# A planned attention-and-FFN kernel: the plan's count for transposing DMAs, and a new order of loads and bursts

## The chip, the cores and the metric

The kernel runs on one core of one Trainium2 chip. The metric is the device time of one execution in microseconds (us), the median of several runs. A profile of one of these executions gives the times of single instructions.

## The reference

Two layers follow each other: an attention whose softmax is replaced by a squared ReLU, and a gated FFN.

```python
B, H, S, D = 8, 12, 448, 64
scores = (q @ k.transpose(0, 1, 3, 2)) / sqrt(D)
attn = maximum(scores, 0) ** 2 / S
x = (attn @ v).transpose(0, 2, 1, 3).reshape(3584, 768)
gate = maximum(x @ w_gate, 0)          # w_gate, w_val: 768 x 1536
val = x @ w_val
out = (gate * val) @ w_out             # w_out: 1536 x 768; out: 3584 x 768, float32
```

## The kernel before, in words

All matrix work is done in bf16 with float32 sums in PSUM. The attention goes by quads: four heads of one batch, so three quads a batch and 24 in all. A quad needs q and k with the head dimension on partitions. For batch 0 (L494, L501) and batch 1 (L527) PE transposes them. For batches 2 to 7 it goes through DMA: a raw tile is loaded from DRAM by a queue that POOL issues (L394), one engine copies it into a permuted tile (L550, mostly DVE), and SP issues two transposing DMAs from there into a tile qkT (L556). There is one raw tile and one permuted tile. So the next raw load waits for the copy before it, and the next copy waits for the two transposes before it.

The scores of a quad are made in steps (L622), four 64x64 matmuls a step that run side by side in the four quarters of the array. ACT or DVE applies the ReLU (L631, L633) and the square (L643, L645). Then PE makes attention times v (L661, 28 matmuls; "PV"), and a copy (L676) puts the result into xT, the FFN's input.

The FFN of batches 0 and 1 is plain: 30 blocks of a gate product and a value product (L721, six matmuls each), a ReLU on ACT (L729) and a multiplication on DVE that writes hT (L731). From batch 2 on, and for every output product, pairs of batches are multiplied by a Strassen scheme with seven products instead of eight (L821 for gate and value, L936 for the output). It needs sums and differences of the weights, which DVE makes once: L744 and L749 from the gate and value weights, L761 from the output weights, into tiles woT and wo. The scheme also needs copies of partial results, tiles f (L770, L772), which DVE adds in again (L849, L871, L887, L926). Results leave through tiles o and DMAs that SP issues (L908).

No loop runs in this order. The function `plan` (L161) takes the operations of all stages and simulates the engines with fixed costs; what it starts first is emitted first. Each engine then runs its instructions in that order, and an instruction that waits holds up all behind it on the same engine. PE's operations come in two lists, `att` and `ffn`, each with its own order, and the planner mixes them: a run of attention between FFN products is a burst here. It starts one when the FFN work done since has reached a share (`START`, or `LATEST` at the latest) of what the ratio of the two lists asks for. While PE waits in the first 21 us, the planner puts in filler matmuls (L1065) whose results nobody reads. POOL's loads have a fixed order, spelled by `ORDER`: V is v of batch 0, L the late part of its q, a digit a pair of gate and value columns, a letter of abcxyz a quad of batches 1 and 2 with its v, a letter of opqr a quarter of w_out.

The planner has one number for the DMA queue, `dmaq`: the time at which it comes free. A load adds its transfer time. A transposing operation (`xbar`) adds a constant, and its end is bounded from the queue's:

```python
if op.xbar:
    self.dmaq = max(self.dmaq, s) + 1.5
    op.end = max(op.end, min(self.dmaq + 2.0, s + 13.0))
```

`LATE` is added to that end for whoever uses the result. `BUFFERS` gives the numbers of the tiles qkT, at, xT, f, g, o and vv.

Of the kernel before, what the change touches and what calls it, by code (L numbers as in the profile page):

```python
# [15 lines left out]
class Res:  # L16


    def __init__(self, n):
        self.free = {i: 0.0 for i in range(n)}  # L20
# [35 lines left out]
class Planner:  # L56
# [1 line left out]
    SWITCH = 0.1  # L58
    BIAS = 0.2
    MARGIN = 4.0  # L60
    LATE = 3.0
    RESERVE = (1000.0, 12.0, 2.0)
    FILL_FROM = 0.4
    FILL_COLD = 4.0
    FILL_UNTIL = 21.0
    FILL_MARGIN = 0.1
    WINDOW = 5
    ATT_WINDOW = 2
    START = 0.8
    LATEST = 3.0  # L70
    HOLD = 0.1
    SLACK = 0.1
    CUTS = ((1, 3), (0, 1, 3, 5, 6), (2, 6), (2, 6))
    GV_ORDER = '1256734'
    OUT_ORDER = 'ab1cd572364'
    END_ORDER = ('517364', '523')
    BUFFERS = (3, 11, 3, 5, 4, 5, 3)
    PV_AT_0 = 1
    QT = 3
    PART = 6  # L80
    PV_AT = 1
    T_AT = 3
    MORE_UNTIL = 4
    BY_PE = 6
    ORDER = 'VL102acbx34y5zroqp'

    def __init__(self, banks):
        self.banks = banks
        self.t = {}
        self.ops = []  # L90
        self.mode = None
        self.dmaq = 0.0
        self.landed = []
# [7 lines left out]
    def ready(self, op):  # L101
        r = 0.0
        for d in op.deps:
            if d.end is None:
                return None
            if d.eng != "PE" or "PE" not in op.engs:
                r = max(r, d.end + (self.LATE if d.xbar else 0.0))
        for b in op.alloc:
# [22 lines left out]
    def commit(self, op, s, e):  # L131
        op.start, op.eng = s, e
        occ, busy = op.engs[e]
        now = self.now(op)
        self.t[e] = s + occ
        op.end = s + busy
        if e == "PE":
            self.mode = op.mode
        if op.load:
            self.dmaq = max(self.dmaq, s + occ + 0.3) + op.load  # L140
            op.end = self.dmaq + 2.0
            self.landed.append(op.end)
        op.end += op.land
        if op.xbar:
            self.dmaq = max(self.dmaq, s) + 1.5
            op.end = max(op.end, min(self.dmaq + 2.0, s + 13.0))
        for b in op.alloc:
            b.idx = b.pick(now)[1]
            for w in range(b.width):
                del b.res.free[b.idx + w]  # L150
            b.last = op.end
        for b in op.reads:
            b.readers -= 1
            b.last = max(b.last, op.end + (self.LATE if op.land else 0.0))
            if b.readers == 0:
                for w in range(b.width):
                    b.res.free[b.idx + w] = b.last
        self.ops.append(op)


def plan(first, att, ffn, others, pool, goals, filler, banks):  # L161
# [33 lines left out]
    def fits(ops, now):  # L195

        among, width = ops[0].alloc[0].among, ops[0].alloc[0].width
        times = sorted(max(P.free_at(i + w) for w in range(width)) for i in among)
        for o, t in zip(ops, times):
            if t > now + P.SLACK:  # L200
                return False
            now += o.engs["PE"][0]
        return True

    first = [list(x) for x in first]
    while any(first) or att or ffn or active or pi < len(pool):
# [18 lines left out]
        else:  # L225
            A = F = None
            for i, op in enumerate(att[:P.ATT_WINDOW]):
                b = P.best(op)
# [10 lines left out]
            elif A is not None and F is not None:  # L239
# [3 lines left out]
                else:  # L243
                    n = next((i for i, o in enumerate(att) if o.cut), len(att) - 1) + 1
                    if debt >= P.LATEST * n * share:
                        pick = "A" if A[0] <= F[0] + 0.15 else "F"
                    elif debt >= P.START * n * share and A[0] <= now + 0.15 and fits(att[:n], now):
                        pick = "A"
# [50 lines left out]
def kernel(  # L299
# [40 lines left out]

    N_QT, N_AT, N_X, N_F, N_G, N_O, N_VV = Planner.BUFFERS
    N_RAW, N_PERM = 1, 1
# [194 lines left out]
    def transpose_dma(b, g):  # L537
        st = quads[(b, g)]
        st.qt_buf = Buf(r_qt)

        pb = Buf(r_perm)
        perm = Op({"DVE": (0.65, 0.72), "ACT": (2.1, 2.2)}, None, deps=st.qk_ops, alloc=[pb],
                  reads=[st.raw_buf] if st.raw_buf else [])

        def emit_perm():
            src = st.raw().rearrange("p (j h) t d -> p j t h d", j=2)
            if perm.eng == "ACT":
                nc.scalar.copy(perm_t[pb.idx], src)
            else:
                nc.vector.tensor_copy(perm_t[pb.idx], src)  # L550

        perm.emit = emit_perm

        def emit():
            for a in range(2):
                nc.sync.dma_start_transpose(out=qkT_t[st.qt_buf.idx][:, a].rearrange("p j (t c) -> p (j t) c", c=P2),  # L556
                                            in_=perm_t[pb.idx][64 * a:64 * a + 64].rearrange("p j t h d -> p (j t h d)"))

        op = Op({"SP": (2.6, 2.6)}, emit, deps=[perm], alloc=[st.qt_buf], reads=[pb])
        op.land = 7.4 if b == 2 else 5.4  # L560
        op.xbar = True
        st.qt_ops = {0: [op]}
        others.extend([perm, op])
# [515 lines left out]
    out_of = dict(zip("opqr", [(par, hf) for par in range(2) for hf in range(2)]))  # L1079
    for x in Planner.ORDER:  # L1080
        if x in "VL":
# [19 lines left out]
    def T(n):  # L1101
        if n < Planner.BY_PE:
            att.append(transpose_pe(*divmod(n, NQ)))
        elif n < B * NQ:
            transpose_dma(*divmod(n, NQ))

    def PV(n):
        att.append(A_[n].pv())
        if A_[n].g == NQ - 1:
            done_at[A_[n].b] = len(att)  # L1110
# [10 lines left out]
    for n in range(NQ, len(A_)):  # L1121
# [3 lines left out]
        for i in range(len(A_[n].steps)):  # L1125
            att.append(A_[n].s(i))
            if i == (Planner.PV_AT if n >= 2 * NQ else Planner.PV_AT_0) and n not in (NQ, 2 * NQ):
                PV(n - 1)
            if i == Planner.T_AT and n >= 2 * NQ - 1:
                T(n + 1 - NQ)  # L1130
# [51 lines left out]
```

## Time and profile before

| What | Value |
|---|---|
| median of 6 runs | 412.7 us |
| lowest and highest run | 410.65 and 415.64 us |
| the profiled execution | 415.3 us, with a span of 413.5 us from first to last instruction |
| PE busy | 398.3 us (96% of the span), 3481 matmuls |
| DVE busy | 324.4 us (78%) |
| ACT busy | 257.3 us (62%) |
| POOL busy | 74.2 us (18%) |
| loads' queue | 23.60 MB, 43.6% of 16 engines' span |
| stores' and transposes' queue | 19.08 MB, 27.9% |
| transposing DMAs | 36, two for each of 18 quads; issue to landing 3.3 / 6.6 / 14.4 us (least, median, most) |

Lines such as L821 are lines of the kernel before. "PE ps L821" is a matmul there that writes the tile ps. "A <- B" means that A waited and B ended the wait. A busy PE in this profile is not a PE at its peak: matmuls are pipelined and overlap in the record, so what one of them takes is read from the length of a row of them.

### The profile page before, as it was taken

The numbers are of one execution on the slowest core, as the hardware profiler recorded it, in microseconds if no ns is written. First come the engines' busy times: TensorE is split into PE (matmuls) and PEld (weight loads), VectorE is DVE, ScalarE is ACT, GpSimd is POOL, SyncE is SP. The second block draws the span as 40 slices with busy tenths as digits, with TensorE's granted clock in tenths as the row PEclk, the third lists the DMA queues.
The fourth block names the chain that finished last, engine by engine and source line by source line (L and its number), as shares of the span: only waits on it lengthen the run. The fifth ranks groups of instructions, "written<-read, shape, count | busy, mean of one in ns | idle before, by whom it ended". The sixth has DMA issues, their size and how long they took to land.

```text
span 413.5 us, 8787 instructions
## 1 busy us (share of the span) xinstructions
PE 398.3 (96%) x3481; PEld 207.0 (50%) x3481; DVE 324.4 (78%) x573; ACT 257.3 (62%) x385; POOL 74.2 (18%) x119
## 2 busy tenths in 40 slices
PE   8979999979999999999999999999999999999995
PEld 4567644433455544444545544444445555555563
DVE  3697979957899988899698699898788757767652
ACT  3888878543677777788587389756575544343221
POOL 7827405201211222221112022210000000000000
PEclk9999999998999999999999999999999999999998
DMA  8999999996479999766879699831002440000144
GB/s 110 189 198 202 179 135 153 176 158 90 69 90 184 142 192 145 104 72 92 101 90 158 124 189 135 111 38 31 2 0 65 99 106 2 1 0 2 38 110 120
DMA packets 75736, 43.43 MB, mean 105 GB/s; under 512 B 37808, under 2 KB 75696, under 8 KB 75696
## 3 DMA queue, kind: packets, MB, share of 16 engines
q0 software_dynamic: 33328, 23.60, 43.6%
q1 hardware_dynamic: 42208, 19.08, 27.9%
q8 instruction: 27, 0.44, 0.5%
q10 hardware_dynamic: 160, 0.20, 0.1%
q14 instruction: 13, 0.11, 0.1%
HBM read 47.19 MB, written 11.01 MB: 141 GB/s over the span
## 4 chain that ended last, share of the span: by engine, by line
PE 78%; DMA 10%; issue 4%; DVE 3%; POOL 2%; ACT 1%; DVEq 0%; POOLq 0%
PE ps L821 35%; PE ps L936 23%; PE ps L622 7%; PE ps L661 6%; PE ps L721 6%; DMA wo<-in_moe_w_out_dram 5%; DMA wg<-in_moe_w_gate_dram 2%; DMA gvT<-in_k_dram 2%; POOL gvT L394 1%; DMA raw<-in_k_dram 1%; DVE at L633 1%; DVE at L645 1%; ACT at L631 1%; POOL wo L394 1%; DMA out_dram<-o 1%
## 5 line engine op out<-in xcount | busy, mean ns | idle before, releaser
L631 ACT ACTIVATE at<-ps 128x896 bf16<-128x896 f32 (+3 forms) x111 | 97.4, 911 | 21.1 <-PE ps L622 20.7
L770 ACT COPY f<-ps 128x448 f32<-128x448 f32 x99 | 51.8, 532 | 47.0 <-PE ps L821 45.6
L633 DVE TENSOR_SCALAR at<-ps 128x896 bf16<-128x896 f32 (+4 forms) x60 | 63.0, 1051 | 12.1 <-PE ps L622 11.6
L645 DVE TENSOR_TENSOR at<-at 128x896 bf16<-128x896 bf16 (+4 forms) x118 | 69.4, 610 | 4.0 <-ACT at L631 3.5
L821 PE MATMUL ps<-xT,gvT 128*128 128x448 bf16 x216 | 52.6, 353 | 0.0
L643 ACT ACTIVATE at<-at 128x896 bf16<-128x896 bf16 (+4 forms) x53 | 49.7, 939 | 4.1 <-DVE at L633 3.4
L821 PE MATMUL ps<-sx,wv 128*128 128x448 bf16 x216 | 52.2, 353 | 0.0
L622 PE MATMUL ps<-qkT 64*64 64x448 bf16 (+2 forms) x756 | 49.7, 337 | 2.1 <-DMA qkT<-perm 1.1
L821 PE MATMUL ps<-xT,wg 128*128 128x448 bf16 x216 | 51.6, 353 | 0.0
L821 PEld LDWEIGHTS <-gvT 128*128 128x128 bf16 x324 | 30.4, 98 | 32.0 <-issue 5.4
L936 PE MATMUL ps<-wo,hT 128*128 128x384 bf16 x240 | 43.9, 326 | 0.1
L936 PEld LDWEIGHTS <-hT 128*128 128x128 bf16 x312 | 29.7, 98 | 22.9 <-issue 3.9
L394 POOL DMA_DIRECT2D vv<-in_v_dram x44 | 26.7, 621 | 77.9 <-PE ps L622 75.4
L936 PEld LDWEIGHTS <-sh 128*128 128x128 bf16 x288 | 27.0, 98 | 21.3 <-issue 3.7
L721 PE MATMUL ps<-xT,wg 128*128 128x448 bf16 (+2 forms) x180 | 33.6, 324 | 4.2 <-DVE hT L731 3.8
L772 ACT ACTIVATE f<-ps 128x384 f32<-128x384 f32 x39 | 19.0, 491 | 28.6 <-PE ps L936 28.6
L661 PE MATMUL ps<-at,vv 64*64 64x448 bf16 (+2 forms) x700 | 33.7, 329 | 0.0
L721 PE MATMUL ps<-xT,wv 128*128 128x448 bf16 (+2 forms) x180 | 32.8, 319 | 0.8 <-DVE at L633 0.8
L394 POOL DMA_DIRECT2D raw<-in_k_dram x18 | 11.3, 628 | 117.6 <-DVE perm L550 98.9
L861 DVE TENSOR_TENSOR hT<-ps,g 128x448 bf16<-128x448 f32 x36 | 22.4, 622 | 12.1 <-PE ps L821 12.1
L676 ACT CAST xT<-ps 128x896 bf16<-128x896 f32 (+2 forms) x27 | 22.2, 821 | 14.8 <-PE ps L661 13.0
L622 PEld LDWEIGHTS <-qkT 64*64 64x64 bf16 x756 | 17.5, 105 | 27.4 <-issue 21.9
(63 smaller groups left out, 484.6 us busy)
## 6 DMA issues: line engine op xcount, KB each, us to landing
out_dram<-o SPq DMA_DIRECT2D x110, 96.0 KB, 2.2
vv<-in_v_dram POOLq DMA_DIRECT2D x44, 112.0 KB, 6.1
raw<-in_k_dram POOLq DMA_DIRECT2D x18, 224.0 KB, 5.1
raw<-in_q_dram POOLq DMA_DIRECT2D x18, 224.0 KB, 6.7
wg<-in_moe_w_gate_dram POOLq DMA_DIRECT2D x6, 384.0 KB, 9.6
wv<-in_moe_w_val_dram POOLq DMA_DIRECT2D x6, 384.0 KB, 10.9
wo<-in_moe_w_out_dram POOLq DMA_DIRECT2D x4, 576.0 KB, 15.8
gvT<-in_k_dram POOLq DMA_DIRECT2D x6, 224.0 KB, 6.4
```

The lines of the kernel that those rows point to most:

```text
L394: op = Op({"POOL": (0.5 + 0.0004 * n_desc,) * 2}, lambda: nc.gpsimd.dma_start(out=dst(), in_=src), deps=deps, alloc=alloc)
L622: nc.tensor.matmul(banks()[64 * j:64 * j + 64, z, h2], lhsT=self.k_of(j, h2, k), rhs=self.q_of(j, h2), start=True, stop=True)
L631: nc.scalar.activation(self.at_of(i, m), banks(), AF.Relu)
L633: nc.vector.tensor_scalar_max(self.at_of(i, m), banks(), 0.0)
L643: nc.scalar.activation(a, a, AF.Square)
L645: nc.vector.tensor_tensor(a, a, a, ALU.mult)
L661: nc.tensor.matmul(ps[64 * h2:64 * h2 + 64, ps2.idx + j, :n], lhsT=st.v_of(j, h2, c), rhs=self.at_of(c)[64 * j:64 * j + 64, 0, h2], start= ...
L721: nc.tensor.matmul(ps[:, pb.idx, :n], lhsT=w[:, kd, fc], rhs=xT_t[xbuf[b].idx][:, kd, cols], start=(kd == 0), stop=(kd == KD - 1))
L770: nc.scalar.copy(dst, src)
L821: nc.tensor.matmul(ps[:, pb.idx, :S], lhsT=w(g)[:, fc], rhs=rhs, start=start and g == 0, stop=stop and g == KH - 1, skip_group_check=True)
L861: h0 = Op({"DVE": V448}, lambda pb=prev["A"], gb=prev["g0b"], mf=prev["mf"]: nc.vector.tensor_tensor(h_slot(b, mf), ps[:, pb.idx, :S], g_t ...
L936: nc.tensor.matmul(ps[:, pb.idx, :OH], lhsT=lhs(kf), rhs=rhs(kf), start=start and kf == 0, stop=kf == FH - 1, skip_group_check=True)
```

## The change

The constants for the transposing DMAs are new, and the plan's other constants are set anew: how bursts are started (`ATT_WINDOW`, `START`, `LATEST`), when PE's transposes stand among the score steps (`T_AT`), the numbers of the tiles, and the order of the loads. POOL is taken as free from 1.25 us on. The arithmetic that the kernel does is the same. Below L142 the lines of the changed kernel are one higher.

```diff
-    LATE = 3.0
+    LATE = 2.0
...
-    ATT_WINDOW = 2
-    START = 0.8
-    LATEST = 3.0
+    ATT_WINDOW = 3
+    START = 0.9
+    LATEST = 1.8
...
-    BUFFERS = (3, 11, 3, 5, 4, 5, 3)
+    BUFFERS = (3, 11, 3, 3, 5, 5, 4)
...
-    T_AT = 3
+    T_AT = 0
...
-    ORDER = 'VL102acbx34y5zroqp'
+    ORDER = 'LV021abc3x4yo5zqpr'
...
-        self.t = {}
+        self.t = {"POOL": 1.25}
...
         if op.xbar:
-            self.dmaq = max(self.dmaq, s) + 1.5
-            op.end = max(op.end, min(self.dmaq + 2.0, s + 13.0))
+            queued = self.dmaq > s + 2.1
+            op.end = max(op.end, min(self.dmaq + 12.0, s + 15.5)) if queued else op.end
+            self.dmaq = max(self.dmaq, s) + (4.5 if queued else 2.5)
...
-        op.land = 7.4 if b == 2 else 5.4
+        op.land = 5.4
```

In the emitted program this changes the order of instructions on every engine: PE has 106 bursts where it had 90, and 49 fillers where it had 37. PE's order is the same again once 366 of the 756 matmuls of L821 are done.

## The prediction

> **What bounds the kernel now.** I read the engines by stage first, cut where the order of work changes: the opening, batches 0 and 1 with the loads, attention between FFN products, FFN alone, the last store. The columns are the stretch, its length, busy us of PE, weight loads, DVE, ACT and POOL, the granted PE clock, and the DMA engines' busy share with GB/s.
>
> ```profile
> 0.00:36.55 36.55, 32.01 (x618) 21.62 (x619) 23.61 (x51) 25.84 (x40) 23.07 (x40) 1.00 1.21 171
> 36.55:117.20 80.65, 74.81 (x703) 38.40 (x703) 67.32 (x100) 52.20 (x73) 21.55 (x32) 0.98 1.15 141
> 117.20:337.80 220.60, 220.60 (x1767) 108.47 (x1767) 189.47 (x343) 153.26 (x224) 29.55 (x48) 1.00 0.67 103
> 337.80:408.70 70.90, 70.89 (x396) 38.55 (x394) 43.97 (x81) 25.50 (x49) 0.00 (x0) 1.00 0.15 38
> ```
>
> From 117 us PE never idles: only PE's own work can be saved there. All that a better plan can win lies before. The waits say where: "who <- whom: us, times, longest".
>
> ```profile
> DVE woT L761 <- DMA wo<-in_moe_w_out_dram: 4.6, 1, 4.6
> ...
> PE ps L721 <- DVE hT L731: 3.8, 1, 3.8
> ...
> PE ps L622 <- DMA qkT<-perm: 1.1, 1, 1.1
> ...
> PE ps L622 <- DVE at L633: 0.7, 1, 0.7
> ```
>
> The first two are one event. The chain shows it (start, length, what):
>
> ```profile
> 68.03 22.48 DMA wo<-in_moe_w_out_dram
> 90.60 1.37 DVE woT L761
> ...
> 93.27 0.63 DVE hT L731
> 93.94 4.09 PE ps L721 x12
> 98.03 0.50 PE ps L622 x8
> 98.54 2.38 PE ps L721 x12
> ```
>
> The last output weight takes 22.48 us to land; DVE stands 4.6 us at L761 waiting for it, the product hT (L731) is queued behind, and PE has no free bank for 3.8 us. Then the same twelve matmuls take 4.09 us where a warm pair of blocks takes 2.38: a second loss of 1.7. The granted clock in that stretch was 0.58:
>
> ```profile
> 93.94:98.03 4.09, 4.09 (x16) 1.59 (x19) 3.55 (x4) 0.54 (x1) 1.24 (x2) 0.58 0.12 20
> ...
> 275.50:279.30 3.80, 3.80 (x44) 1.94 (x44) 3.58 (x7) 2.12 (x3) 1.20 (x2) 1.00 1.04 119
> ```
>
> The second row is for the change's main number: there the two transposes of the last quad are alone in the queues. They move 2 x 64 x 1792 x 2 bytes = 459 KB and hold all engines for 3.8 us.
>
> Last, what a burst of attention costs PE between FFN products:
>
> ```profile
> 250.20 1.81 PE ps L821 x9
> 252.01 0.50 PE ps L622 x8
> 252.51 2.38 PE ps L821 x12
> ...
> 337.78 45.97 PE ps L821 x243
> ```
>
> Undisturbed, 243 matmuls take 0.189 us each. Nine then need 1.70 and take 1.81; twelve need 2.27 and take 2.38; eight 64x64 matmuls (two rounds of four in parallel) need 0.38 and take 0.50. So one burst, in and out, costs 0.11 + 0.12 = 0.23 us, whatever is in it.
>
> **The change, part by part.** All edits but the buffers act through the order of instructions, so I count in the two orders.
>
> *The counted transposes.* The plan had 1.5 us of DMA queue for a quad's pair and now has 2.5, or 4.5 behind loads; the row above says 3.8 alone. This moves no byte; it makes the plan expect qkT and the weights later and put other work in front. The pages have a rule against it: the Trainium skill, "DMA: Bandwidth & Descriptors", section "Latency and other measured facts", gives DMA transposes an effective 261 GB/s; by it a pair would need an estimated 1.8 us, the old count would be nearly right and the new order needlessly careful. The row shows 119 GB/s, and the row decides.
>
> *The stall on the output weights: -5.5 us.* On DVE the first L761 moves from behind the product of gate/value block 22 (of 30) to behind that of block 23, with its attention step; one more product stands between the first two L761. On POOL one of the four wo loads moves ahead of the last gate/value pair, the other three stay behind the last raw quad of batch 2. Up to that product PE has 1.7 us more work (block 2.27, less attention before it), one burst (0.2) and some 1 us from the opening (below). So DVE comes to L761 at about 86.0 + 2.9 = 88.9, and PE runs dry near 92.7. The loads ahead of the last wo are the same, so I let it land within 3 us of 90.5: L761 and the next product (1.36 + 0.62) are then done by 92.5, inside PE's cover. I take the whole 3.8 + 1.7 = 5.5. Bounds: 0 (lands 4 us later) to -5.5.
>
> *The first transposed quad: -0.9.* Its raw load moves behind the third gate/value pair (4 us of queue in the trace: landed 43.2 to 47.2), so its perm copy (L550) and SP's two transposes move from 46 to about 50. The next raw load, and with it wo on POOL, waits for that copy, as 98.9 us of POOL's waits do now. PE asks for this quad at block 15 as before, but with 1.3 us more work and the longer opening in front: about 64.4 instead of 62. In the trace these transposes landed 10.8 and 14.3 us after issue; from 50 that is 64.3. So some of the 1.1 + 0.7 us stays; I take half of 1.9 away. Bounds: -1.9 to +3 (L550 queues in front of an L731 again, and the next quad behind this one).
>
> *More bursts: +3.7.* In the new order PE changes between attention and FFN 212 times instead of 180: 106 bursts for 90. Twelve of the sixteen stand in the Strassen product of batches 2 and 3 (32 bursts for 20, seventeen of them of a single 4-matmul step), three before. 16 x 0.23 = 3.7. PE is full there, so nothing hides it. Bounds 2.8 (four of them in waits) to 3.9.
>
> *The opening: +1.0.* Late q is loaded before v; v had over 4 us to spare before its first use at 16.7 and loses about 2, late q gains. Eight new fillers, 8 x 0.18 = 1.4 us, stand between the first two products, and the scores that now start at 20.2 come after the value product, whose weight landed at 21.6: they start near 22.3. From there to the state both orders share (six blocks, 45 score slots, six PV) the new order has 12.6 us of matmuls and eleven changes (1.3): 36.2 at best, against 36.5 now; the waits of the old order there (0.8, 0.6, 0.5, 0.3 us, on ACT and DVE) make it 37.5 if most return, since both engines are over 8/10 busy. Bounds 0 to +2. Four more fillers at the start end before or just after the load PE waits for (0.53 idle at 5.98); 0.5 at most, and later fillers take it up.
>
> *Buffers: +0.3.* Three f tiles for five: of 148 writes to f in the trace one, at 156, found three others still in use, for 1.3 us. Between 0 and 1.3; ACT waits 45.6 us for PE at L770 and covers most. One more vv and g: POOL's 75.4 us at vv shrink, and nobody waits for POOL then. SP's stores keep their places among the transposes but for a few; five o tiles stay. From the last 243 products on, the order is the same.
>
> **The sum.** -5.5 - 0.9 + 3.7 + 1.0 + 0.3 = -1.4 on the profiled execution's 415.3 (span 413.5 and 1.8 around it): 413.9. That execution lies 2.6 over the median, and the runs spread over 5 us. The matmuls can't differ, so I ascribe the spread to waits on DMA. If all 2.6 is the stall that goes, 413.9 stands for the median too; if it is something else, 411.3. I take the middle, 412.6, against 412.7.
>
> **The rivals.** What can be told from no change here is 1%: under 408.6 is faster, over 416.8 slower.
>
> *Forecast, 0.53:* the stall goes and the bursts eat it. Own range 410 to 415.5.
>
> *Transposes take the stall's place, slower, 0.22.* Place: the first quad of batch 2. Behind its issue at 50 now queue a raw quad with v (3.4), a wo (3.0) and a gate/value pair (4.2), 10.6 us, and its own 7.1 (the engine time of the pair in the loaded stretch 46 to 62). In sequence that is 17.7: landed 67.7, for PE at 64.4, and DVE's next L550 waits with products behind it. A wait of 3.3, the kept 0.9, and 1.7 of clock if PE rests as long as at 90: 412.6 + 5.9 = 418.5. It decides from a landing 17 us after issue. For it: the queue is full until 90. Against: the longest landing in the trace is 14.4 us.
>
> The clock's part has a rule of its own: the Trainium skill, "TensorE: Matmul & The Clock Gate", section on the HAM clock gate, lets the clock halve after an idle window of about 3.4 us. The rows: 0.58 after 3.8 us idle, 1.00 after the waits of 1.1 and 0.7. By the page a 3.3 us wait could go without the 1.7.
>
> *The change doesn't do what it says, slower, 0.05:* three wo loads still come last, behind a perm that is later, and land at 95: 412.6 + 4 = 416.6 or more.
>
> *Single-step bursts choke, slower, 0.06:* each of 17 waits 0.25 us for DVE or ACT: +4.3, 416.9. DVE is at 9/10 there. Against: PE waits nowhere there now, and bursts leave both engines 2.8 us more time.
>
> *All waits go, faster, 0.14:* the other 0.9 at the quad, the opening 1.3 better than I have it, four bursts inside waits (0.9), on the lower base: 411.3 - 3.1 = 408.2.
>
> Range 408.5 to 418.
>
> **What would show it.** Right: L761 idles under 1 us; PE has no idle over 3 us after 36 us; the clock is 1.00 in every stage; 106 bursts at 0.23; the stage from the first output product to 337 of matmuls longer by about 3 us. Wrong: PE idle on qkT over 3 us near 65, wo landing after 94, or PE idle at L622 between 120 and 185.

## The result, and the profile after

The changed kernel takes 414.9 us, the median of 34 runs (413.13 to 417.32); 71 runs of the kernel before beside it have a median of 412.3 (408.32 to 417.36). The ratio is 1.0077, 95% interval 1.0062 to 1.0092; it leaves out runs over 1.5% above the fastest of their kernel, and with them the longest executions of before. By it the change costs 0.8%: 414.9 / 1.0077 = 411.8 for the kernel before, 3.2 us less (2.6 to 3.8); over all runs the two medians differ by 2.7 and the two means by 2.2. Forecast was 412.6, level. The profiled execution took 413.4 us with a span of 411.6.

The stages first, by the columns of the prediction, but cut at points of the work that both kernels share: the end of the sixth block of gate and value (72 matmuls of L721, L722 after), of the 30th, of the 366th matmul of L821 (L822), and the last matmul. The profiled execution before, its second and third stage (the first took 35.9 us, the last 134.8):

```profile
35.90:115.40 79.50, 73.72 (x700) 37.87 (x701) 66.01 (x98) 51.05 (x71) 21.97 (x33) 0.98 1.15 142
115.40:273.90 158.50, 158.43 (x1298) 76.72 (x1299) 140.10 (x254) 117.20 (x168) 28.35 (x46) 1.00 0.85 124
```

The one after, all four:

```profile
0.00:34.80 34.80, 31.83 (x593) 21.43 (x593) 22.09 (x47) 24.17 (x38) 22.81 (x39) 1.00 1.22 173
34.80:107.90 73.10, 72.47 (x713) 37.67 (x716) 60.93 (x92) 51.69 (x74) 19.55 (x30) 1.00 1.09 146
107.90:271.90 164.00, 162.50 (x1315) 76.18 (x1318) 136.88 (x251) 120.98 (x176) 31.12 (x52) 1.00 0.82 120
271.90:406.80 134.90, 134.86 (x886) 71.05 (x886) 94.83 (x176) 63.34 (x107) 0.44 (x1) 1.00 0.24 49
```

The second stage is 6.4 us shorter than in the long execution of before that the prediction was read from, and its clock is whole; the third is 5.5 longer, with the clock at 1.00 in both. In the waits of PE (who, whom, us, times, longest) the 3.8 us at hT are gone:

```profile
PE ps L623 <- DMA qkT<-perm: 1.3, 2, 0.9
...
PE ps L722 <- ACT at L632: 0.5, 1, 0.5
PE ps L822 <- ACT o L773: 0.4, 1, 0.4
```

The output weights, seen by their tile (issues, then least, median and longest time to land) and on DVE's timeline:

```profile
L395 POOL DMA_DIRECT2D wo<-in_moe_w_out_dram x4: 886/899/909, 54.0 to 68.3; - x4
...
DMA to landing us min/median/max: 9.2/12.4/15.6
```

```profile
88.70 1.35 DVE L762 TENSOR_TENSOR woT<-wo 128x2304 bf16<-128x2304 bf16 x1
89.97 0.62 DVE L732 TENSOR_TENSOR hT<-ps,g 128x448 bf16<-128x448 f32 x1
90.50 1.35 DVE L762 TENSOR_TENSOR woT<-wo,woT 128x2304 bf16<-128x2304 bf16 x1
```

The last of them is there by 68.3 + 15.6 = 83.9 at the latest, where in the profile before it landed at 90.5; DVE comes to L762 at 88.7 and doesn't wait.

The kernel before has more than one kind of execution, and that decides how the first number is read. Two more profiles of it took 415.95 and 411.25 us. Their waits of PE on hT, in this order:

```profile
PE ps L721 <- DVE hT L731: 4.0, 1, 4.0
```

```profile
PE ps L721 <- DVE hT L731: 1.2, 1, 1.2
```

The second stage of the execution of 411.25 us, with its clock:

```profile
35.30:110.30 75.00, 72.02 (x700) 37.37 (x704) 65.71 (x98) 51.04 (x71) 21.86 (x33) 1.00 1.18 152
```

That is 75.0 us for the 79.5 of the execution that I summed from. Two kernels of the experiments below, burst_price and burst_control, have the same order of PE as before up to the last stage; their waits on hT, in this order:

```profile
PE ps L721 <- DVE hT L731: 0.4, 1, 0.4
```

```profile
PE ps L721 <- DVE hT L731: 1.6, 1, 1.6
```

So in five profiles of this order the stall was 3.8, 4.0, 1.2, 0.4 and 1.6 us. Two more profiles of the kernel after (414.6 and 415.2 us) agree with the first within 1 us in each stage: 34.8 and 35.1, 74.0 and 73.9, 164.4 and 164.8, 134.9.

### The profile page after: what moved, and what is told of

Read it like the earlier page. It is cut to its first block, busy times and chain, and to the rows that moved or that the text cites. A ratio compares the mean times of both kernels' runs of the same rounds, so it can differ in the third digit from the quotient of the medians.

```text
span 411.6 us, 8805 instructions
## 1 busy us (share of the span) xinstructions
PE 401.7 (98%) x3493; PEld 206.3 (50%) x3493; DVE 314.7 (76%) x564; ACT 260.7 (63%) x394; POOL 73.9 (18%) x119
## 4 chain that ended last, share of the span: by engine, by line
PE 81%; DMA 11%; DVE 3%; ACT 2%; issue 1%; POOL 1%; SPq 0%; DVEq 0%; ACTq 0%; POOLq 0%
PE ps L822 32%; PE ps L937 22%; PE ps L722 11%; PE ps L623 8%; DMA qkT<-perm 7%; PE ps L662 6%; DMA out_dram<-o 2%; DMA gvT<-in_q_dram 1%; PE ps L1066 1%; ACT at L632 1%; DVE at L646 1%; POOL gvT L395 1%; DVE at L634 1%; ACT at L644 0%; DVE o L927 0%
## 5 line engine op out<-in xcount | busy, mean ns | idle before, releaser
L632 ACT ACTIVATE at<-ps 128x896 bf16<-128x896 f32 (+4 forms) x119 | 104.5, 911 | 17.4 <-PE ps L623 16.9
L771 ACT COPY f<-ps 128x448 f32<-128x448 f32 x101 | 53.0, 533 | 46.0 <-PE ps L822 40.2
L634 DVE TENSOR_SCALAR at<-ps 128x896 bf16<-128x896 f32 (+4 forms) x52 | 55.0, 1060 | 11.1 <-PE ps L623 10.8
L822 PE MATMUL ps<-xT,gvT 128*128 128x448 bf16 x216 | 52.8, 353 | 0.0
L623 PE MATMUL ps<-qkT 64*64 64x448 bf16 (+2 forms) x756 | 50.9, 339 | 1.5 <-DMA qkT<-perm 1.3
L822 PE MATMUL ps<-xT,wg 128*128 128x448 bf16 x216 | 51.4, 353 | 0.4 <-ACT o L773 0.4
L822 PE MATMUL ps<-sx,wv 128*128 128x448 bf16 x216 | 51.8, 353 | 0.0
L644 ACT ACTIVATE at<-at 128x896 bf16<-128x896 bf16 (+4 forms) x52 | 48.3, 939 | 3.4 <-DVE at L634 3.0
L822 PEld LDWEIGHTS <-gvT 128*128 128x128 bf16 x324 | 29.8, 98 | 32.0 <-issue 6.7
L722 PE MATMUL ps<-xT,wg 128*128 128x448 bf16 (+2 forms) x180 | 32.5, 316 | 0.6 <-ACT at L632 0.5
L862 DVE TENSOR_TENSOR hT<-ps,g 128x448 bf16<-128x448 f32 x36 | 22.4, 622 | 13.7 <-PE ps L822 13.6
L927 DVE SCALAR_TENSOR_TENSOR o<-ps,f 128x384 f32<-128x384 f32 x40 | 22.2, 554 | 13.6 <-PE ps L937 13.4
L722 PE MATMUL ps<-xT,wv 128*128 128x448 bf16 (+2 forms) x180 | 32.2, 315 | 0.1
```

Of the source, the lines that this page charges most:

```text
L623: nc.tensor.matmul(banks()[64 * j:64 * j + 64, z, h2], lhsT=self.k_of(j, h2, k), rhs=self.q_of(j, h2), start=True, stop=True)
L632: nc.scalar.activation(self.at_of(i, m), banks(), AF.Relu)
L634: nc.vector.tensor_scalar_max(self.at_of(i, m), banks(), 0.0)
L644: nc.scalar.activation(a, a, AF.Square)
L722: nc.tensor.matmul(ps[:, pb.idx, :n], lhsT=w[:, kd, fc], rhs=xT_t[xbuf[b].idx][:, kd, cols], start=(kd == 0), stop=(kd == KD - 1))
L771: nc.scalar.copy(dst, src)
```

## The experiments

Each row below is one kernel: median, ratio to the kernel before with its interval, then from its profile the four stages (us), the changes of PE between attention and FFN within the third, and the waits there. The waits, cold clock included, are an estimate: what the third stage has over the 158.5 us of before (158.9 and 159.5 in its two other profiles), less 0.117 us for each change above 90, and less the matmuls that the order moves into the stage. Those are priced by the rows of undisturbed matmuls in the prediction (0.189 us for 448 columns, in proportion for others, a quarter of it for one of four that run side by side): 0.8 us in after, a_late3 and a_late3_o6, -0.4 in b_window3, 0.2 in a_window2, 4.0, 3.0 and 2.5 in b_dma_count, b_count_late3 and a_late4_w2.

| kernel | median | ratio, 95% | stages | changes | waits |
|---|---|---|---|---|---|
| after | 414.9 | 1.0077 (1.0062 to 1.0092) | 34.8 / 73.1 / 164.0 / 134.9 | 118 | 1.4 |
| b_wo_later | 410.3 | 0.9975 (0.9944 to 1.0006) | 35.0 / 73.5 / 158.3 / 134.8 | 89 | 0 |
| b_window3 | 411.6 | 0.9999 (0.9964 to 1.0035) | 36.1 / 72.7 / 159.6 / 135.0 | 105 | 0 |
| a_window2 (profile of its longest execution, 420.75) | 416.9 | 1.0102 (1.0053 to 1.0152) | 34.8 / 80.4 / 164.1 / 134.8 | 89 | 5.5 |
| b_dma_count | 420.3 | 1.0194 (1.0152 to 1.0237) | 35.5 / 69.7 / 173.5 / 132.5 | 102 | 9.6 |
| a_late3 | 416.3 | 1.0106 (1.0051 to 1.0161) | 34.4 / 73.7 / 166.3 / 135.0 | 119 | 3.6 |
| b_late2 | 416.6 | 1.0100 (1.0042 to 1.0159) | 35.2 / 80.5 / 159.5 / 134.8 | 89 | 1.1 |
| b_count_late3 | 418.5 | 1.0163 (1.0109 to 1.0218) | 35.6 / 69.7 / 171.7 / 134.3 | 93 | 9.9 |
| burst_price | 420.4 | 1.0183 (1.0126 to 1.0240) | 37.4 / 72.3 / 158.6 / 143.1 | 90 | 0 |
| burst_control | 412.5 | 1.0013 (0.9980 to 1.0045) | 35.0 / 75.0 / 158.6 / 135.7 | 90 | 0 |
| a_late3_o6 | 414.0 | 1.0043 (1.0016 to 1.0070) | 35.1 / 73.7 / 164.0 / 135.0 | 119 | 1.3 |
| a_late4_w2 | 425.3 | 1.0300 (1.0257 to 1.0343) | 35.0 / 73.0 / 174.8 / 134.2 | 91 | 13.7 |

### What the stall was worth: b_wo_later

The kernel before with one more dependency in the plan: L761 may start only after the product of block 25.

```diff
-    To_ops = make_To()
+    To_ops = make_To([ffn[2 * 25 - 1][0]])
...
-                    deps=list(wo_op.values()) + res[-1:])
+                    deps=list(wo_op.values()) + res[-1:] + list(after))
```

> The kernel before, where the planner may start the four L761 only after the value product of block 25; loads as before. They move from behind blocks 22, 22, 23, 24 to behind 24, 25, 25, 26; 91 bursts. If the stall is worth 5.5 us in a usual execution as in the profiled one (the prediction's term): ratio 0.987 to 0.990, about 407. If the profiled execution was unlucky and the stall is worth 1 to 3 us in the median: ratio 0.993 to 0.998, and the spread of the runs shrinks as the slowest fall away. In the profile PE shows no wait over 1 us between 80 and 100 us.

Its waits of PE show the stall all but gone, with 0.6 us on a quad, at 90 us, beside it:

```profile
PE ps L622 <- DMA qkT<-perm: 0.6, 1, 0.6
...
PE ps L721 <- DVE hT L731: 0.3, 1, 0.3
```

By the ratio that is 1.0 us (the interval reaches from 2.3 us less to 0.2 more), by the medians of all runs 1.4, by their means 1.8; by none is it 5.5. Its twelve runs lie between 408.3 and 412.0, where the 23 runs of the kernel before beside them reach from 407.2 to 417.9. So the stall of 4 us with its cold clock belongs to long executions of the kernel before (415.3 and 415.95 us); in the other three profiles of its order it is short. It is the best version that these runs give, but its interval does not exclude no change.

### What a burst costs by itself: burst_price and burst_control

In the kernel before, 32 empty bursts are put between the products of L821 in blocks 2 to 9 of the last pair of batches, where there is no attention. Each is four 64x64 matmuls of 64 columns into a bank that the next product overwrites. The control has one 128x128 matmul of 64 columns at the same places.

```diff
+                if b == B - 2 and 2 <= mf <= 9 and n in (1, 2, 5, 7):
+                    for h2 in range(2):
+                        for j in range(2):
+                            nc.tensor.matmul(ps[64 * j:64 * j + 64, h2, :64], lhsT=vv_t[0][64 * h2:64 * h2 + 64, 0, j, :],
+                                             rhs=vv_t[0][64 * h2:64 * h2 + 64, 1, j, :], start=True, stop=True)
```

```diff
+                if b == B - 2 and 2 <= mf <= 9 and n in (1, 2, 5, 7):
+                    nc.tensor.matmul(ps[:, 0, :64], lhsT=vv_t[0][:, 0, 0:2, :].rearrange("p c d -> p (c d)"),
+                                     rhs=vv_t[0][:, 1, 0, :], start=True, stop=True)
```

> The kernel before with 32 empty bursts where PE is full and nothing else waits: in the last FFN stage, ahead of products 1, 2, 5 and 7 of blocks 2 to 9, four 64x64 matmuls of 64 columns each, side by side, into banks that nobody reads. If a change of the array's form costs 0.117 us, a burst 0.23: 32 x (0.23 + 0.03) = 8.4 us more in the stage from the 366th product of L821 to the end (134.8 before), ratio 1.018 to 1.022. If bursts are nearly free in a full PE and the stage with attention is longer for other reasons: under 3 us.

> The control of burst_price: at the same 32 places one 128x128 matmul of 64 columns, the same streaming time without the change of form. 32 x 0.03 = 0.9 us more, at most 2 if short matmuls cost extra; ratio 1.001 to 1.005. The difference of the two is the price of 32 bursts, 7.4 us if the prediction's 0.23 holds.

The chain of each (start, length, what), first with empty bursts (L822) between the products (L826), then with the control's matmul (L820) between them (L824):

```profile
350.65 0.15 PE ps L822 x4
350.81 1.24 PE ps L826 x6
```

```profile
351.55 0.03 PE ps L820
351.58 1.14 PE ps L824 x6
```

The stage from the 366th product on, of each:

```profile
267.20:410.30 143.10, 143.10 (x1015) 72.03 (x1014) 96.77 (x176) 63.60 (x107) 1.20 (x2) 1.00 0.18 39
```

```profile
264.60:400.30 135.70, 135.70 (x916) 71.72 (x915) 97.47 (x179) 63.78 (x108) 1.20 (x2) 1.00 0.18 40
```

Six matmuls take 1.24 us after a burst and 1.14 after a plain matmul; the four small ones take 0.15 for 0.03. Over the whole stage it is (143.1 - 135.7) / 32 = 0.23 us a burst, the prediction's figure, and it shows in the time: the ratios are 1.0183 and 1.0013, some 7 us apart. Two changes to a burst make about 0.117 each. The Trainium skill, "TensorEngine Tiling (Array Packing)", section "Key Properties", says that a change of tiling mode drains TensorE. The rows agree: the change costs time, 0.23 us for in and out.

### Bursts alone: a_window2 and b_window3

ATT_WINDOW alone decides most of the number of bursts. The first is the kernel after with the old value (90 bursts), the second the kernel before with the new one (101).

```diff
-    ATT_WINDOW = 3
+    ATT_WINDOW = 2
```

```diff
-    ATT_WINDOW = 2
+    ATT_WINDOW = 3
```

> The changed kernel with one constant put back: ATT_WINDOW 2 instead of 3. The order falls back from 106 bursts to 90; loads, transposes, buffers, opening and fillers stay those of the changed kernel, and the first L761 stands behind block 22, the next behind 23 and 24. Theory 'bursts' (16 more bursts at 0.23 us are the loss, and the stall on the output weights is worth far less than 5.5 us in a usual execution): 3.7 us off the changed kernel, so about 411.2, a ratio to the kernel before of 0.995 to 1.000. Rival 'late transposes' (waits for qkT in the stage with attention are what costs): the transposes stay as late, so at most 1 us off, about 414, ratio 1.005. Rival 'opening' (the fillers and late scores cost 2 us or more): about 413, ratio 1.002 to 1.004, and the first stage in the profile still ends later than in the kernel before.

> The kernel before with ATT_WINDOW 3 instead of 2 and nothing else. The order has 101 bursts for 90; three of the four L761 now stand behind block 22, one behind 23, so the stall on the output weights stays or grows. Theory 'bursts': 11 x 0.23 = 2.5 us more, ratio 1.005 to 1.008. Rivals 'late transposes' and 'opening': neither loads nor opening change, so no more than 0.5 us, ratio 0.999 to 1.001, unless the stall itself grows, which the profile would show at L761.

Neither went as bursts alone would have it. b_window3 has 15 changes more in the third stage, 1.8 us, and that stage is 1.1 longer; but no wait on hT appears in its profile, and its second stage is 72.7 us for the 75.0 to 79.6 of before (that profile is of one of its fastest executions, 409.94 us). In sum it is level, within 1.4 us; by what its second stage gains in the median is not settled, since two of its twelve runs lie at 415.5 and 416.0 again. a_window2 has 29 changes fewer than after, 3.4 us, and is not faster. Its order of work waits in other places; how long in a usual execution is not shown, since the profile is of its longest, 3.9 us over its median:

```profile
PE ps L623 <- DMA qkT<-perm: 3.1, 4, 1.6
PE ps L722 <- DMA wv<-in_moe_w_val_dram: 2.7, 1, 2.7
...
PE ps L937 <- DVE o L927: 1.9, 2, 1.6
```

### The count for the queue alone, and the slack: b_dma_count, b_count_late3, b_late2, a_late3

The kernel before with the changed count, POOL's start and LATE 2; the same with LATE 3 kept; the kernel before with LATE 2 alone; the kernel after with LATE 3 alone. The last two are one line each. The first:

```diff
-    LATE = 3.0
+    LATE = 2.0
...
-        self.t = {}
+        self.t = {"POOL": 1.25}
...
-            self.dmaq = max(self.dmaq, s) + 1.5
-            op.end = max(op.end, min(self.dmaq + 2.0, s + 13.0))
+            queued = self.dmaq > s + 2.1
+            op.end = max(op.end, min(self.dmaq + 12.0, s + 15.5)) if queued else op.end
+            self.dmaq = max(self.dmaq, s) + (4.5 if queued else 2.5)
...
-        op.land = 7.4 if b == 2 else 5.4
+        op.land = 5.4
```

> The kernel before with the DMA count of the change alone (queue share of transposes 2.5 or 4.5, their ends, LATE 2, POOL free from 1.25), old order of loads, old buffers and bursts constants. 92 bursts; the L761 move to behind blocks 24, 25, 25, 26. This is the part that the change is named for. Theory 'bursts': two bursts more (0.5 us) and the stall gone, so as b_wo_later plus 0.5, ratio 0.994 to 1.000. Rival 'late transposes': if planning for slower transposes itself makes PE wait or makes worse mixtures, ratio 1.003 or more, with idle PE at the scores after 110 us.

> The kernel before with the new DMA count, the new landing constant and POOL's start, but LATE 3 as before: b_dma_count with one constant put back. 89 bursts; L761 behind blocks 24, 25, 26, 26. 'Slack': the 3.7 us of waits for qkT of b_dma_count go and its time falls from 1.019 to 1.000 or below, 0.994 with the gain at the output weights. Rival 'the count itself': the new share and ends of queued transposes make a worse plan whatever LATE is: ratio stays over 1.010, and PE still waits at the scores between 110 and 235 us.

> The kernel before with LATE 2 instead of 3 and nothing else; 91 bursts, first L761 still behind block 22. 'Slack': the plan uses a quad at 10 us instead of 11, so waits for qkT appear after 111 us, 1 to 3 us, ratio 1.002 to 1.008. 'Bursts': one more, 0.2 us, ratio 1.000. 'Loads': nothing, 1.000.

> The changed kernel with LATE 3 again instead of 2: the plan lets PE use a transposed quad one us later. Loads, opening and the DMA count stay; 108 bursts. New theory 'slack' (the new constants let the plan use a quad 8 + 2 = 10 us after SP's first transpose where the traces show 8.4 to 11.1, so PE now waits for qkT in the stage with attention): the waits for qkT after 111 us (0.9 us in the changed kernel's profile, 2.3 to 3.7 in the two slower ones) go, 1 to 3 us off, ratio to the kernel before 1.000 to 1.005. Rival 'bursts': two more bursts, 0.5 us more, ratio 1.008 to 1.010. Rival 'opening or loads': no change, 1.007.

b_dma_count is 1.9% slower than before with 102 changes in the third stage for after's 118: with the old loads and bursts the count does more harm than the whole change does. In both kernels with the count the greatest wait is of PE on a quad that has not landed. First b_dma_count, then b_count_late3:

```profile
PE ps L623 <- DMA qkT<-perm: 5.1, 3, 2.8
```

```profile
PE ps L623 <- DMA qkT<-perm: 4.4, 2, 3.7
```

So the slack alone is not the cause: 1 us of LATE returned, and a wait of 3.7 us remains. In the kernel before, without the count, LATE 2 alone does it too, and 6.0 of the 7.0 us fall on quads of batch 2 (at 58 and 94 us):

```profile
PE ps L622 <- DMA qkT<-perm: 7.0, 3, 4.0
```

And in after, LATE 3 shortens the waits on quads (0.9 us in sum for 1.3 to 2.7) and is not faster: 1.0106 beside 1.0077. A different wait appears, which the prediction had at nothing. The waits of PE, then the chain, of a_late3:

```profile
PE ps L937 <- DVE o L927: 2.2, 1, 2.2
```

```profile
223.96 1.82 SPq L557
...
225.88 0.53 SPq L909
...
226.46 7.94 DMA out_dram<-o
...
234.52 0.57 DVE o L927
```

The store (L909) is issued right behind the two transposes of a quad (L557) and lands after 7.94 us. The page's part on DMA issues has the median of this kernel's stores:

```profile
out_dram<-o SPq DMA_DIRECT2D x110, 96.0 KB, 2.3
```

DVE has no free o tile in that time. Its timeline, with the idle time and its releaser in brackets:

```profile
234.52 0.56 DVE L927 SCALAR_TENSOR_TENSOR o<-ps,f 128x384 f32<-128x384 f32 x1 [4.93 <-DMA out_dram<-o]
```

### One more o tile: a_late3_o6

To see whether that wait is the tile's, a_late3 with six o tiles. PE's order is that of a_late3.

```diff
-    BUFFERS = (3, 11, 3, 3, 5, 5, 4)
+    BUFFERS = (3, 11, 3, 3, 5, 6, 4)
```

> a_late3 with six o tiles instead of five; PE's order is the same. In a_late3 PE stood 2.2 us at 233 us because DVE waited 4.9 us for a store that was queued behind two transposes (7.9 us to landing). Theory 'stores behind transposes': one more tile takes most of it, PE's wait there falls under 1 us and the time by 1 to 2 us, ratio 1.004 to 1.009. If the wait has another cause: unchanged, 1.010.

The wait is gone and the third stage is 164.0 us for 166.3; the ratio falls from 1.0106 to 1.0043 (1.0016 to 1.0070). So the wait was for an o tile, and one tile more took its 2.3 us. That the store was late because of the transposes ahead of it is read from the chain and not tested by itself. What is left in the third stage is 119 changes and 1.3 us of small waits, and the kernel is still slower than before.

### More slack and fewer bursts at once: a_late4_w2

If bursts and slack were all, LATE 4 with the old ATT_WINDOW should have come out level with before or under it.

```diff
-    LATE = 2.0
+    LATE = 4.0
...
-    ATT_WINDOW = 3
+    ATT_WINDOW = 2
```

> A try for a better version: the changed kernel with LATE 4 (a quad is used 12 us after its first transpose at the earliest, over the longest 11.1 measured) and ATT_WINDOW 2 (88 bursts). Opening and loads of the change stay. If the loss is bursts and late quads together: no wait for qkT over 0.5 us after 111 us, the stage from block 30 to the 366th product 159 to 160 us instead of 164 to 165, the whole 408 to 410, ratio 0.992 to 0.997. If each new order brings waits of its own, whatever the constants: 162 or more there, ratio over 1.000.

It is the slowest of all, with 91 changes in the third stage, one more than before, and 13.7 us of waits, on a quad, on DVE and on o:

```profile
PE ps L623 <- DMA qkT<-perm: 2.6, 1, 2.6
PE ps L822 <- DVE at L634: 2.3, 1, 2.3
...
PE ps L937 <- DVE o L927: 1.2, 2, 0.9
```

Each new order brings waits of its own. Eight kernels in the table have another count, LATE or order of loads than before; all eight wait in the third stage, for 1.1 to 13.7 us. The order of before, and the four that leave these three alone, wait there for 0.9 us at most: 0.3 and 0.9 us in two of the three executions of before, nothing in the other profiles. The 1.1 us of b_late2 are hardly more than that.

### The kernels themselves again

The two more profiles of each kernel, told of with the result, were taken to learn how much a single execution is worth.

> The kernel before, unchanged, one more execution. If the stall on the output weights is a matter of luck (the runs with a granted clock of 0.993 or less are the slow ones, about one in five): PE idle on hT near 90 us is under 1.5 us, the clock stays 1.00 there, and the stage from block 6 to block 30 takes 73 to 76 us instead of 79.5. If the stall is usual: 3 to 4 us again. After 117 us no wait over 0.5 us in any case.

> As before_look1: one more execution of the kernel before, to see how far its stages vary. Luck: stall under 1.5 us. Usual: 3 us or more.

> The changed kernel, unchanged, one more execution; its first profile is among its fastest runs. If waits in the attention stage are the loss: the stage from block 30 to the 366th product of L822 is longer than the 164.0 us of the first profile by 1 to 3 us, with waits for qkT or for stores, while opening and loads stay within 0.5 us. If the extra bursts alone are the loss: 164 again, waits under 1.5 us.

> As after_look1: one more execution of the changed kernel. Waits: 165 to 167 us in that stage; bursts alone: 164.

The kernel before gave two kinds, with the stall (415.95 us) and nearly without (411.25), and the last output weight landed at 91.2 and 87.1 us. The 0.9 us that PE waited on a quad at 154 us in the execution of 411.25 were not expected. The three of after lie within 1.9 us; the third stages of the two new ones, 164.4 and 164.8, are 0.4 and 0.8 us longer than the first, less than the 1 to 3 us expected for waits. Why the weight lands 4 us later in one execution than in the other is not settled: the four loads were issued 1.3 us later in the long one.

## Why the prediction was wrong

**The stall: the term that failed.** "I take the whole 3.8 + 1.7 = 5.5" was right of the execution that it was read from: L762 came to its turn at 88.7 (predicted 88.9), no wait was left and the second stage lost 6.4 us. But it stood against the median, and there the stall is not 5.5. The profile of 411.25 us has 1.2 with no loss of clock, and b_wo_later puts the stall's whole worth at 1.0 to 1.8 us (its interval reaches from nothing to 2.3). The text had the warning, 2.6 us between its execution and the median, and named the answer for the case that it is the stall: 413.9. "I take the middle, 412.6" gave half of it away. Even 413.9 is 1.0 short of 414.9; the waits below are large enough for that rest. One premise failed without harm: "The loads ahead of the last wo are the same, so I let it land within 3 us of 90.5". It landed by 83.9, so in this execution DVE would not have waited at its old turn of 86.0 either; the later turn was not what removed the stall there. Why the weight came 6.6 us earlier is not settled.

**The bursts: right.** 32 changes more in the whole, at 0.117 measured by itself: 3.7 us, as predicted. 28 of them, 3.3 us, stand in the third stage and nothing hides them there; with 1.4 us of waits and 0.8 us of attention put off from the opening it is longer by 5.5, not by the 3 that I said.

**The waits of the new order: costed at 0.3, measured 1.4 to 2.2.** Two sentences failed. The count "makes the plan expect qkT and the weights later" holds only for a queue that is busy. For a quad whose queue is free the plan now has the quad ready 2.6 + 5.4 + 2 = 10 us after the start of its transposes, where it was 11 or more. The chain of after shows the second transpose of a pair that took longer than PE was given, and the timeline the idle PE behind it:

```profile
174.42 9.78 DMA qkT<-perm
```

```profile
184.24 0.57 PE L623 MATMUL ps<-qkT 64*64 64x448 bf16 x8 [0.92 <-DMA qkT<-perm]
```

"SP's stores keep their places among the transposes but for a few; five o tiles stay" was the other. In the chain of after one store takes 7.09 us and PE waits 0.4 behind ACT's o:

```profile
137.85 7.09 DMA out_dram<-o
...
145.04 0.50 ACT o L773
```

Such a store is not new: the slowest store of before takes 7.9 us. There PE never waits behind one; in the new order it does.

The prediction had named "PE idle at L622 between 120 and 185" as a sign that it is wrong. It came, at 184.

**The first transposed quad: right.** -0.9 predicted. PE waited 1.1 and 0.7 us near 62 and 65 before (0.9 and 0.7 in the execution of 411.25 us) and 0.4 to 1.1 near 64 after.

**The opening: smaller.** +1.0 predicted. It ends 0.2 to 0.5 us earlier than in the execution of 411.25 us, but with 0.8 us of attention put off to the third stage: 0.3 to 0.6 in all.

**The sum, made again** on the typical execution of before, 411.25 us: stall -1.2, first quad -1.3 to -0.5, bursts +3.7, opening +0.3 to +0.6, waits +0.4 to +1.2 (1.4 to 2.2, less 1.0 that this execution's own third stage, 159.5 us, has over 158.5). That is +1.9 to +3.8; the three profiled executions of after are 2.1 to 4.0 us longer than this one, and the ratio gave 3.2. I have not measured each of these in an execution of its own: the price of a burst is shown by an experiment, the stall by one whose interval just reaches nothing, and the wait on o in a_late3 by another; the first quad, the opening and the waits of after itself are read from the profiles alone.

**The rivals.** Transposes did not take the stall's place at 64; a wait of 3.3 us on them appeared nowhere in after. That the change doesn't do what it says fell: the stall is gone. Single-step bursts did not choke. "All waits go" fell too.

## What to carry to other kernels

Before a stall is booked as a gain, look at a second and a third execution of the kernel: a stall at the end of a DMA race can be 4 us in one and 1 in the next, and only its mean is to be won. Constants meant to tell a planner more of a queue need not make a better order: the count alone cost 1.9% here. Where the order of before hardly waits in a stage, a new order there has little to win and waits to lose, and extra changes of tiling mode are paid in full where PE is busy throughout. When transposes and stores share a queue, ask of each store that follows a pair of transposes how many output tiles are left.

## What the runs showed of the hardware

A wait of PE need not reach 3.8 us to cost the clock. In a_window2 the 2.74 us at L722 did it. PE's timeline, and the 3 us from there and 1 us later by the columns of the stages (the granted clock is the third number from the end):

```profile
74.00 2.42 PE L722 MATMUL ps<-xT,wv 128*128 128x448 bf16 x6 [2.74 <-DMA wv<-in_moe_w_val_dram]
```

```profile
74.00:77.00 3.00, 3.00 (x9) 1.22 (x10) 1.42 (x2) 0.00 (x0) 0.00 (x0) 0.50 1.26 188
78.00:79.00 1.00, 1.00 (x7) 0.51 (x6) 0.96 (x2) 0.54 (x1) 0.00 (x0) 1.00 1.31 202
```

In before, after 3.8 us, the clock was at 0.50 from 93.9 to 97.3, and the half of these 3.4 us is the second loss of 1.7 that the prediction read there.

After the 2.23 us in a_late3, at 235, it stayed whole:

```profile
235.10:238.10 3.00, 2.97 (x18) 1.66 (x17) 2.47 (x5) 0.49 (x1) 0.79 (x2) 1.00 0.61 145
```

b_dma_count after 2.82 us (0.50 for 3 us) and b_late2 after 2.02 us (1.00) say the same. But the length of one wait doesn't draw the line. In a_late4_w2 the clock was whole through a wait of 2.28 us and fell to one half 0.6 us after it; it fell again at 159.0, behind two waits of 0.95 and 0.81 us:

```profile
148.12 0.73 PE L822 MATMUL ps<-xT,wg 128*128 128x448 bf16 x3 [2.28 <-DVE at L634]
...
156.67 0.59 PE L623 MATMUL ps<-qkT 64*64 64x448 bf16 x8 [0.95 <-DVE at L634]
```

```profile
145.30:148.70 3.40, 1.03 (x11) 0.40 (x6) 3.40 (x6) 3.40 (x6) 0.00 (x0) 1.00 1.36 166
148.80:155.50 6.70, 4.10 (x45) 1.99 (x45) 3.28 (x6) 2.61 (x4) 2.44 (x4) 0.50 0.85 86
155.60:158.90 3.30, 1.54 (x19) 0.64 (x15) 3.30 (x7) 3.03 (x5) 0.00 (x0) 1.00 1.31 143
159.00:162.30 3.30, 3.30 (x10) 1.29 (x9) 1.49 (x4) 2.12 (x4) 0.00 (x0) 0.50 0.89 153
```

So these runs show waits that cost the clock and waits that don't, and no edge between them. The Trainium skill, "TensorE: Matmul & The Clock Gate", section "Part 1: The HAM clock gate", has the half rate come after at least one idle window of about 3.4 us; here waits shorter than that window sufficed, and the measurement decides.

A store of 96 KB that lands in 2.2 us by the median took 7.1 and 7.9 us when it was issued behind a pair of transposes on the same queue. That transposes are the only cause is not shown: in the kernel before, stores that SP issued between 237 and 247 us, with no transpose among them, took up to 7.1 us as well.
